# Three weight loads of the first dense layer asked for between the tiles of the attention's start

## The chip, the cores and the metric

The kernel runs on one core of one Trainium2 chip. The metric is the time of one execution on the device, in microseconds (us), the median of the runs shown. The core has a matrix engine (PE, with its weight loads as PEld), a vector engine (DVE), a scalar engine (ACT), a general engine (POOL) and a sync engine (SP), which here issues every transfer. Each engine takes its instructions from one queue, in order.

## The reference

An attention with 32 memory slots per head, then two dense layers, all in float32 (the weights of the dense layers come as float64):

```python
a = softmax(phi)                                  # (8, 8, 576, 32), over the 32 slots
k_m, v_m = a^T k, a^T v                           # (8, 8, 32, 64)
attn = softmax(q k_m^T / 8)                       # (8, 8, 576, 32)
x = (attn v_m) as (4608, 512)
h = max(x w1, x w2, x w3)                         # moe1: w1..w3 are 512 x 768
x = h w_out                                       # 768 x 512
x = (sigmoid(x w_gate) * (x w_val)) w_out         # moe2: 512 x 1536, 512 x 1536, 1536 x 512
```

## The kernel before

**The tiles.** The 8 x 8 heads are cut into 16 attention tiles, n = 2b + g: batch b, half g of the heads. Two batches make a pass p, so the first four tiles (n = 0 to 3) belong to pass 0. A tile goes through six stages, one generator each: `a0` (softmax of phi, begun), `a1` (it is transposed on PE), `a2` (k_m and v_m, PE matmuls at L209 from the tile's phi, k and v), `a3` (transposes at L228, then the splits into `vt` on ACT and DVE), `a4` (q k_m^T at L246, two halves of q; DVE transposes the scores at L256 and takes their maximum; POOL subtracts it, ACT takes the exponential) and `a5` (sum, division, transposed back into `stg`).

**The dense layer moe1.** Its weights w1, w2, w3 lie in `wx` as J = 6 column blocks of four row blocks (j, hp), 24 pieces of 128 x 384 float64, called w0 to w23 here in the order in which they are used (the fourth to sixth are w3, w4, w5). The values of v_m are multiplied into the weights first (`g_step`, PE at L343, results `g` split by ACT and DVE or POOL), and the attention is then multiplied with that (`h_step`, PE at L370).

**A weight's way.** `w_want` asks for a piece (tile `raw`, three buffers, 384 KB each). `w_have` turns it into float32 (`w_f32`, L123 to L129: two operations on ACT, three on DVE), splits it into a high and a low part (`w_split`: L134 on ACT, L73 on POOL) and stores both in `wxs` for the later passes (384 KB again). `w_step` asks for the next piece and then does `w_have` for the oldest one asked for; `wq` holds those asked for.

**What sets the order.** The first pass has a list `acts` of what is done ahead of step t of the first four tiles. Its transfers stay on SP in the order in which the program names them (`dma` with `queue["in order"]`); the other engines' instructions are put in order by a scheduler that works through a timeline of its own. All SP transfers share eight semaphores, so a transfer is issued when the one eight places ahead has landed. Tiles `early` (phi, q, k, v of the first tiles) have buffers of their own; from q of tile 1 on, `q` has three buffers.

After the list, the rest of the weights is stepped through at fixed places of the loop over pass 0 (`at(4 * (j - 2) + hp, w_step)`), beside `g_step` and `h_step`. After pass 0 there are three more passes, and then moe2.

Of the kernel before, what the change touches and what calls it, by code (L numbers as in the profile page):

```python
# [18 lines left out]
def attn_moe_kernel(  # L19
# [274 lines left out]
    def w_want(j, hp, p):  # L294
        if p == 0:
            wq.append((j, hp, p, w_fetch(mid, wx[j, hp] if j >= 0 else wo1[hp])))
        else:
            t = mid.tile([128, 2, PC], F32R, tag="wx", name="wx", bufs=6)
            dma(f32(t), wxs[j, hp])
            wq.append((j, hp, p, t))  # L300

    def w_have():
        j, hp, p, w = wq.pop(0)
        if j < 0:
            w = w_f32(mid, w)
            r = slice(hp * PC, hp * PC + PC)
            w_split(w, wo1_t[:, 0, r], wo1_t[:, 1, r])
            return
        if p == 0:
            w = w_f32(mid, w)  # L310
            t = mid.tile([128, 2, PC], F32R, tag="wx", name="wx", bufs=6)
            w_split(w, t[:, 0], t[:, 1])
            dma(wxs[j, hp], f32(t))
            w = t
        WX[j, hp] = w
# [213 lines left out]
    for pos, fn, *a in (  # L529
        (0, lambda: w_want(*w0[0])), (0, lambda: w_want(*w0[1])),  # L530
        (0, load_phi, 0), (0, load_kv, 0), (0, lambda: w_want(*w0[2])),
        (0, load_phi, 1), (0, load_kv, 1),
        (0, load_phi, 2), (0, load_phi, 3), (1, load_kv, 2), (2, load_kv, 3),
        *((n, load_q, n, e) for n in range(4) for e in range(2)),
        *((n + 1, lambda: w_step()) for n in range(4)),
    ):
        acts.setdefault(pos, []).append((fn, a))
    w0 = [(j, hp, 0) for j in range(J) for hp in range(4)]
# [2 lines left out]
    def w_step():  # L541
        if not wq:
            return
        if plan:
            w_want(*plan.pop(0))
        w_have()
# [337 lines left out]
```

## Time and profile before

| | |
|---|---|
| median of 3 runs | 1384.53 us (1384.27 to 1385.37) |
| the profiled execution's own time | 1385.23 us |
| its span | 1383.4 us |
| PE busy | 1336.3 us, 97% of the span |
| DVE busy | 862.3 us, 62% |
| mean granted clock of PE | 0.985 of full speed |

The times of rows are counted from the span's start. A row of the timeline gives start, duration, engine, line, operation, written tile, read tiles, shape and count, and in brackets the idle time of the engine just before it and what ended it. A row of a window gives, for each engine, its busy time there and in brackets how many instructions; PEclk is the granted clock of PE as a share of full speed, and the DMA share is the mean busy share of the 16 transfer engines. A row of several instructions covers the time from the first to the last of them.

### The profile page before, as it was taken

What the parts mean: (1) busy time and instruction counts of PE and PEld (TensorE: products, weight loads), DVE (VectorE), ACT (ScalarE), POOL (GpSimd) and SP (SyncE); (2) the same over time, 40 slices, a digit from 0 to 9 for tenths busy, and PEclk for the clock granted to TensorE, in tenths of its full rate; (3) what the DMA queues carried; (4) which work ended last, traced back from release to release, by engine and by line L of the source; (5) the groups of instructions that cost most, each with busy time, mean ns of one, the idle gap of its engine ahead of it and who ended that gap; (6) DMA issues with size and microseconds to landing.
All of it is one profiled execution on the core that took longest, in us unless ns stands there. A gap on an engine that the chain in (4) does not pass through costs nothing.

```text
span 1383.4 us, 22155 instructions
## 1 busy us (share of the span) xinstructions
PE 1336.3 (97%) x7864; PEld 1184.9 (86%) x7864; DVE 862.3 (62%) x1533; ACT 573.5 (41%) x1220; POOL 517.2 (37%) x454
## 2 busy tenths in 40 slices
PE   6689999998999999999999999999999999999998
PEld 3578899997999899888888888888888899999997
DVE  5999758877876885666665344553444544544454
ACT  5687546546654664453343311333222332233221
POOL 2775422421341228554586111461112711161111
PEclk9799999999999999999999999999999999999999
DMA  9588857579648935965556544565555676566661
GB/s 313 178 274 302 267 163 236 175 230 327 217 129 275 318 105 163 334 256 191 199 205 221 189 158 152 171 214 179 168 179 165 204 238 217 196 228 237 207 216 58
DMA packets 112270, 292.44 MB, mean 211 GB/s; under 512 B 12576, under 2 KB 28960, under 8 KB 112160
## 3 DMA queue, kind: packets, MB, share of 16 engines
q1 hardware_dynamic: 112160, 291.03, 62.5%
q8 instruction: 62, 1.02, 0.3%
q14 instruction: 48, 0.39, 0.1%
HBM read 224.92 MB, written 66.06 MB: 210 GB/s over the span
## 4 chain that ended last, share of the span: by engine, by line
PE 83%; DMA 7%; DVE 5%; ACT 2%; issue 2%; SPq 1%; POOL 0%; DVEq 0%; ACTq 0%
PE po L769 22%; PE px L702 16%; PE ps L370 13%; PE pv L702 10%; PE pz L702 10%; PE ps L393 7%; DMA raw<-wb_dram 3%; PE ps L343 2%; PE ps L246 1%; PE ps L209 1%; DMA raw<-wx_dram 1%; DMA early<-kvt_dram 1%; DVE ca L129 1%; DVE ca L128 1%; DVE g L73 1%
## 5 line engine op out<-in xcount | busy, mean ns | idle before, releaser
L769 PE MATMUL po<-wo,gg 128*128 128x512 f32 x1296 | 327.7, 392 | 1.0 <-POOL gg L73 1.0
L73 POOL TENSOR_TENSOR gg<-gf,gg 128x512 fp32r<-128x512 f32 (+1 forms) x120 | 143.4, 1195 | 468.9 <-ACT gg L735 426.0
L769 PEld LDWEIGHTS po<-wo,gg 128*128 128x128 f32 x1296 | 242.4, 188 | 49.5 <-POOL gg L73 1.3
L370 PE MATMUL ps<-attn,g 128*128 128x288 f32 x1728 | 258.9, 303 | 20.8 <-DVE g L73 9.4
L370 PEld LDWEIGHTS ps<-attn,g 128*128 128x128 f32 x1728 | 246.2, 194 | 30.0 <-POOL g L73 7.5
L702 PE MATMUL px<-xa,tb 128*128 128x512 f32 (+1 forms) x1080 | 243.7, 368 | 0.0
L781 DVE TENSOR_TENSOR acc<-po,acc 128x512 f32<-128x512 f32 x180 | 124.3, 691 | 175.0 <-PE po L769 174.9
L702 PEld LDWEIGHTS px<-xa,tb 128*128 128x128 f32 x1080 | 198.1, 188 | 28.0
L702 PE MATMUL pz<-xa,tb 128*128 128x512 f32 (+1 forms) x720 | 169.0, 367 | 1.1 <-DVE u L753 1.1
L702 PE MATMUL pv<-xa,tb 128*128 128x512 f32 (+1 forms) x720 | 169.2, 367 | 0.0
L393 PE MATMUL ps<-h,wo 128*128 128x288 f32 x1152 | 158.5, 296 | 0.0
L393 PEld LDWEIGHTS ps<-h,wo 128*128 128x128 f32 x1152 | 154.3, 188 | 2.8 <-issue 2.1
L73 POOL TENSOR_TENSOR h<-hm,h 128x288 fp32r<-128x288 f32 x96 | 84.1, 878 | 190.1 <-ACT h L68 98.3
L702 PEld LDWEIGHTS pz<-xa,tb 128*128 128x128 f32 x720 | 132.0, 188 | 20.0 <-issue 1.5
L702 PEld LDWEIGHTS pv<-xa,tb 128*128 128x128 f32 x720 | 131.8, 188 | 17.8
L735 ACT CAST gg<-gf 128x512 fp32r<-128x512 f32 (+1 forms) x120 | 69.4, 578 | 176.0 <-DVE gf L731 131.0
L753 DVE TENSOR_TENSOR u<-pz,p 128x512 f32<-128x512 f32 (+1 forms) x120 | 76.2, 635 | 100.8 <-PE pz L702 96.1
L725 ACT ACTIVATE sg<-sg 128x512 f32<-128x512 f32 (+1 forms) x90 | 53.1, 590 | 145.1 <-DVE sg L723 144.9
L73 DVE TENSOR_TENSOR g<-ps,g 64x384 fp32r<-64x384 f32 x180 | 99.3, 552 | 19.6 <-ACT g L357 16.4
L357 ACT CAST g<-ps 64x384 fp32r<-64x384 f32 x192 | 90.6, 473 | 45.6 <-DVE g L73 28.1
L73 POOL TENSOR_TENSOR xa<-xf,xa 128x512 fp32r<-128x512 f32 (+1 forms) x64 | 78.9, 1254 | 20.4 <-ACT xa L134 20.3
L731 DVE TENSOR_TENSOR gf<-gf,sg 128x512 f32<-128x512 f32 (+1 forms) x90 | 71.0, 789 | 9.9 <-ACT sg L725 1.3
(92 smaller groups left out, 1394.2 us busy)
## 6 DMA issues: line engine op xcount, KB each, us to landing
tb<-tbs SPq DMA_DIRECT2D x168, 512.0 KB, 3.8
wx<-wxs SPq DMA_DIRECT2D x72, 384.0 KB, 4.2
wo<-wos SPq DMA_DIRECT2D x48, 512.0 KB, 5.2
tbs<-tb SPq DMA_DIRECT2D x42, 512.0 KB, 2.9
raw<-wb_dram SPq DMA_DIRECT2D x48, 384.0 KB, 4.5
kv<-kvm_dram SPq DMA_DIRECT2D x48, 256.0 KB, 5.2
raw<-wx_dram SPq DMA_DIRECT2D x24, 384.0 KB, 3.7
wxs<-wx SPq DMA_DIRECT2D x24, 384.0 KB, 4.5
```

The source lines that it names most:

```text
L73: eng.tensor_tensor(out=o, in0=a, in1=b, op=ALU.subtract)
L343: pe.matmul(ps[:, :384], lhsT=vt[:, x, 2 * e:2 * e + 2].rearrange("p a m -> p (a m)"), rhs=w[:, y], start=(n == 0), stop=(n == 2),)
L357: act.copy(t[r, 0], ps[r, :384])
L370: pe.matmul(ps[w][:, :U], lhsT=G[b, j, g][:, x, 128 * w:128 * w + 128], rhs=at[:, y, hf * U:hf * U + U], start=(n == 0), stop=(n == 5),)
L393: pe.matmul(ps[:, :U], lhsT=wo1_t[:, x, (d * J + j) * 128:(d * J + j) * 128 + 128], rhs=H[u, j][:, y], start=(n == 0), stop=(n == 3 * J - 1),)
L702: pe.matmul(ps[:, :half], lhsT=w[:, a, o:o + 128], rhs=x[:, k, c, :half], start=(first and n == 0), stop=(n == 5), skip_group_check=not first,
L725: act.activation(out=sg, in_=src, func=AF.Sigmoid)
L731: vec.tensor_tensor(out=gf, in0=gf, in1=sg, op=ALU.mult)
L735: act.copy(t[:, 0, :half], gf)
L753: vec.tensor_tensor(out=u, in0=ps[:, :half], in1=E["p1", v], op=ALU.add)
L769: pe.matmul(ps, lhsT=GG[sc, j, c, h][:, x, 128 * m:128 * m + 128], rhs=WO[sc, j, h][:, y], start=(n == 0), stop=(n == 5),)
L781: vec.tensor_tensor(out=t, in0=ps, in1=t, op=ALU.add)
```

## The change

Three of the four calls of `w_step` in the list `acts` are moved ahead. The first now stands behind k and v of tile 1, ahead of phi of tiles 2 and 3; the second ahead of k and v of tile 2; the third ahead of k and v of tile 3. The fourth stays behind the loads of q. Each call asks for the next piece, converts the oldest one and stores it, so that loads, conversions and stores move together: w3 is asked for as w0 is converted and stored, w4 with w1, w5 with w2, w6 with w3.

```diff
         (0, load_phi, 0), (0, load_kv, 0), (0, lambda: w_want(*w0[2])),
-        (0, load_phi, 1), (0, load_kv, 1),
-        (0, load_phi, 2), (0, load_phi, 3), (1, load_kv, 2), (2, load_kv, 3),
+        (0, load_phi, 1), (0, load_kv, 1), (0, lambda: w_step()),
+        (0, load_phi, 2), (0, load_phi, 3), (1, lambda: w_step()), (1, load_kv, 2),
+        (2, lambda: w_step()), (2, load_kv, 3),
         *((n, load_q, n, e) for n in range(4) for e in range(2)),
-        *((n + 1, lambda: w_step()) for n in range(4)),
+        (3, lambda: w_step()),
     ):
```

SP's queue behind k and v of tile 1, before (`raw` is a weight's load, `wxs` a weight's store, `early` the first tiles' phi, q, k and v):

```order
L53 DMA early<-phiT_dram 128x576 x2
L53 DMA early<-qT_dram 128x576 x2
L53 DMA early<-kvm_dram 128x512 x4
L53 DMA early<-kvt_dram 64x512
L53 DMA q<-qT_dram 128x576 x2
L53 DMA raw<-wx_dram 128x384
L53 DMA wxs<-wx 128x768
L53 DMA early<-kvm_dram 128x512 x4
L53 DMA early<-kvt_dram 64x512
```

The same place now:

```order
L53 DMA raw<-wx_dram 128x384
L53 DMA wxs<-wx 128x768
L53 DMA early<-phiT_dram 128x576 x2
L53 DMA early<-qT_dram 128x576 x2
L53 DMA raw<-wx_dram 128x384
L53 DMA wxs<-wx 128x768
L53 DMA early<-kvm_dram 128x512 x4
L53 DMA early<-kvt_dram 64x512
L53 DMA q<-qT_dram 128x576 x2
L53 DMA raw<-wx_dram 128x384
L53 DMA wxs<-wx 128x768
L53 DMA early<-kvm_dram 128x512 x4
```

One weight's load and store stood ahead of k and v of tile 3; now there are three loads and three stores.

SP's queue at the last loads of q, now (q_216 and q_218 belong to tile 2, q_264 and q_266 to tile 3; wx_522 is w4 split, wx_547 is w5 split, wx_277 is w3 split; raw_268 is w6):

```order
L53 DMA q_216<-qT_dram 128x576
L53 DMA wxs_58<-wx_522 128x768
L53 DMA q_218<-qT_dram 128x576
L53 DMA q_264<-qT_dram 128x576
L53 DMA wxs_58<-wx_547 128x768
L53 DMA q_266<-qT_dram 128x576
L53 DMA raw_268<-wx_dram 128x384
L53 DMA wxs_58<-wx_277 128x768
L53 DMA raw_513<-wx_dram 128x384
```

The stores of w4 and w5 now stand between the loads of q, the one of w5 directly ahead of the second half of tile 3's q.

DVE's queue, before, from the conversion of w4 to the scores of tile 3 (ca_515 is w4, ca_540 is w5; s_464 are the scores of tile 2, s_493 those of tile 3):

```order
L127 TENSOR_SCALAR ca_515<-ca_515 128x384
L73 TENSOR_TENSOR vt_381<-ps_461,vt_381 128x64
L256 STREAM_TRANSPOSE s_464<-ps_455 128x288
L256 STREAM_TRANSPOSE s_464<-ps_456 128x288
L273 RECIPROCAL sm_448<-sm_448 128x18
L128 ISA ca_515<-ca_515,cr_516 128x768
L261 TENSOR_REDUCE mx_467<-s_464 128x18
L129 SCALAR_TENSOR_TENSOR ca_515<-raw_194,ca_515 128x384
L127 TENSOR_SCALAR ca_540<-ca_540 128x384
L276 STREAM_TRANSPOSE stg_453<-s_429 128x576
L128 ISA ca_540<-ca_540,cr_541 128x768
L129 SCALAR_TENSOR_TENSOR ca_540<-raw_255,ca_540 128x384
```

The rows that stand between w4's new place and w5's last operation, now, in two pieces; first w4 (s_372 are the scores of tile 0):

```order
L200 COPY es_332<-ps_306 64x128
L127 TENSOR_SCALAR ca_515<-ca_515 128x384
L128 ISA ca_515<-ca_515,cr_516 128x768
L129 SCALAR_TENSOR_TENSOR ca_515<-raw_146,ca_515 128x384
L256 STREAM_TRANSPOSE s_372<-ps_335 128x288
```

and then from w5 to the scores of tile 3 (s_429 are the scores of tile 1, g1_527 is a result of `g_step`):

```order
L129 SCALAR_TENSOR_TENSOR ca_540<-raw_193,ca_540 128x384
L271 TENSOR_REDUCE sm_448<-s_429 128x18
L276 STREAM_TRANSPOSE stg_397<-s_372 128x576
L272 TENSOR_SCALAR sm_448<-sm_448 128x18
L273 RECIPROCAL sm_448<-sm_448 128x18
L276 STREAM_TRANSPOSE stg_453<-s_429 128x576
L256 STREAM_TRANSPOSE s_464<-ps_455 128x288
L256 STREAM_TRANSPOSE s_464<-ps_456 128x288
L73 TENSOR_TENSOR vt_381<-ps_461,vt_381 128x64
L261 TENSOR_REDUCE mx_467<-s_464 128x18
L73 TENSOR_TENSOR vt_381<-ps_461,vt_381 128x64
L73 TENSOR_TENSOR g1_527<-ps_551,g1_527 64x384
```

The next row there is the first transpose of s_493. Both conversions that stood between the scores of tiles 2 and 3, or around them, now stand ahead of the scores of tile 2, and one split of `g` has come ahead of the scores of tile 3. On PE, five `g_step` (15 matmuls at L343) now stand between the two halves of tile 3's q product (L246), where there were four (12). The order of the engines differs only in pass 0: PE's queue is word for word the same from about its 322nd row of 2270 to the end (that row lies in the `x2_step` part of pass 0, L393).

## Rows read from the trace of the kernel before

**Rows 1.** The page: busy time of PE and of DVE, and the granted clock of PE, in 40 slices of the span.

```profile
PE   6689999998999999999999999999999999999998
DVE  5999758877876885666665344553444544544454
PEclk9799999999999999999999999999999999999999
```

**Rows 2.** Windows of the whole span.

```profile
0.00:35.00 35.00, 21.85 (x215) 11.74 (x216) 18.55 (x51) 18.86 (x48) 8.07 (x13) 0.90 0.93 311
35.00:137.00 102.00, 82.35 (x550) 74.41 (x547) 100.28 (x185) 77.53 (x183) 70.37 (x63) 0.87 0.75 250
137.00:200.00 63.00, 63.00 (x505) 56.97 (x506) 41.69 (x94) 28.99 (x70) 24.73 (x22) 1.00 0.67 218
600.00:1383.40 783.40, 778.40 (x3653) 671.52 (x3651) 399.63 (x604) 224.45 (x406) 268.58 (x225) 1.00 0.56 192
```

**Rows 3.** Windows of the first 50 us.

```profile
10.00:20.00 10.00, 8.47 (x101) 5.47 (x101) 5.84 (x19) 6.60 (x18) 1.34 (x2) 1.00 1.05 365
20.00:30.00 10.00, 7.13 (x91) 3.37 (x89) 6.07 (x17) 4.24 (x13) 1.78 (x2) 0.89 1.05 348
30.00:35.00 5.00, 4.90 (x29) 1.99 (x22) 1.57 (x4) 2.31 (x7) 2.60 (x3) 0.53 0.65 228
35.00:40.00 5.00, 4.16 (x22) 2.75 (x18) 5.00 (x11) 2.50 (x7) 4.00 (x3) 1.00 0.97 323
45.00:50.00 5.00, 0.61 (x2) 0.64 (x3) 4.94 (x10) 4.83 (x12) 4.42 (x5) 0.50 0.55 215
```

**Rows 4.** The chain that ended last, in order of time, the transfers of the first tiles in it (start, duration, what).

```profile
4.01 6.43 DMA early<-kvt_dram
10.46 5.89 DMA early<-phiT_dram
16.37 6.11 DMA early<-kvt_dram
22.50 7.13 DMA early<-kvm_dram
```

**Rows 5.** Groups of DVE instructions by line from 0 to 34 us, the three of the conversion (busy time, mean ns of one; idle before them and its releaser).

```profile
L128 DVE CUSTOM_DVE_ANT_0 ca<-ca,cr 128x768 uint16<-128x768 uint16 x4 | 2.7, 674 | 0.1
L129 DVE SCALAR_TENSOR_TENSOR ca<-raw,ca 128x384 uint32<-128x384 uint32 x4 | 2.2, 555 | 0.1
L127 DVE TENSOR_SCALAR ca<-ca 128x384 uint32<-128x384 uint32 x4 | 1.4, 358 | 7.1 <-ACT ca L123 7.1
```

**Rows 6.** The same three groups from 34 to 145 us.

```profile
L129 DVE SCALAR_TENSOR_TENSOR ca<-raw,ca 128x384 uint32<-128x384 uint32 x25 | 21.9, 878 | 0.3
L128 DVE CUSTOM_DVE_ANT_0 ca<-ca,cr 128x768 uint16<-128x768 uint16 x25 | 19.4, 779 | 0.2
L127 DVE TENSOR_SCALAR ca<-ca 128x384 uint32<-128x384 uint32 x25 | 17.2, 692 | 0.1
```

**Rows 7.** Timeline of DVE from w4's conversion to the transposes of tile 3's scores and the split after them.

```profile
35.19 0.35 DVE L127 TENSOR_SCALAR ca<-ca 128x384 uint32<-128x384 uint32 x1
35.45 0.22 DVE L73 TENSOR_TENSOR vt<-ps,vt 128x64 fp32r<-128x64 f32 x1
...
36.49 1.35 DVE L128 CUSTOM_DVE_ANT_0 ca<-ca,cr 128x768 uint16<-128x768 uint16 x1
37.77 0.74 DVE L261 TENSOR_REDUCE mx<-s 128x18 f32<-128x576 f32 x1
38.43 0.85 DVE L129 SCALAR_TENSOR_TENSOR ca<-raw,ca 128x384 uint32<-128x384 uint32 x1
39.20 1.31 DVE L127 TENSOR_SCALAR ca<-ca 128x384 uint32<-128x384 uint32 x1
40.43 0.77 DVE L276 STREAM_TRANSPOSE stg<-s 128x576 f32<-128x576 f32 x1
41.13 0.66 DVE L128 CUSTOM_DVE_ANT_0 ca<-ca,cr 128x768 uint16<-128x768 uint16 x1
41.82 1.24 DVE L129 SCALAR_TENSOR_TENSOR ca<-raw,ca 128x384 uint32<-128x384 uint32 x1
42.98 0.83 DVE L256 STREAM_TRANSPOSE s<-ps 128x288 f32<-128x288 f32 x2
43.75 0.51 DVE L73 TENSOR_TENSOR g<-ps,g 64x384 fp32r<-64x384 f32 x1
```

**Rows 8.** Timeline of PE and, at its end, of ACT: tile 3's k and v (L209), its transposes (L228), the q products of tiles 2 and 3 (L246; eight records are a tile's product), the first `g_step` (L343), the first `h_step` (L370), and ACT's copy between L209 and L228; and, at the top, a q product earlier on.

```profile
18.83 1.20 PE L246 MATMUL ps<-early,kt 128*64 128x288 f32 x8
...
29.67 1.40 PE L209 MATMUL ps<-early,es 128*32 128x128 f32 x16
33.11 0.69 PE L228 MATMUL ps<-ident,kvb 128*128 128x128 f32 x2
33.73 1.91 PE L246 MATMUL ps<-q,kt 128*64 128x288 f32 x8
35.57 2.36 PE L343 MATMUL ps<-wx,vt 128*128 128x384 f32 x12
37.86 1.18 PE L246 MATMUL ps<-q,kt 128*64 128x288 f32 x4
...
49.39 2.50 PE L370 MATMUL ps<-attn,g 128*128 128x288 f32 x9 [7.05 <-DVE g L73]
...
31.19 0.63 ACT L218 ACTIVATE kvb<-ps,rm 128x128 f32<-128x128 f32 x2 [1.32 <-PE ps L209]
```

**Rows 9.** SP's queue in the first 62 us: whom its transfers waited for (us in total, times, the longest).

```profile
SPq L53 <- POOL wx L73: 6.4, 3, 3.7
```

## The prediction

> **What bounds the kernel now.** I read the page's slices first. PE is full nearly everywhere; it is not in the first slices, and there DVE stands at 9 [rows 1]. The windows say where the bound changes. From 35 to 137 us DVE is busy for 100.28 of 102 us, and PE for only 82.35; from 137 to 200 us PE is busy for 63.00 of 63, and from 600 us to the end for 778.40 of 783.40 [rows 2]. So there are three stretches: a start of 35 us in which neither is full (DVE 18.55 us of 35, that is 16.45 us idle), a stretch of 102 us that DVE sets, and the rest, which PE sets. What DVE reaches earlier in the second stretch, PE gets earlier, and with the same order of instructions behind it the end comes earlier by as much.
>
> What bounds the start is the third thing to read. The transfer engines show a share of 1.05 from 10 to 30 us, at 365 and 348 GB/s [rows 3], and the chain that ended last is four transfers of the first tiles in a row from 4 to 29.6 us [rows 4]. So the start is set by bytes, and DVE waits for them. The change gives DVE work for this idle time, and puts bytes in front of the tiles to do so. The question is which is larger.
>
> **What is removed.** In the changed order the conversions of w4 and w5 stand ahead of the scores of tile 2; before, they lay on both sides of them. I count what they hold of DVE up to the transposes of tile 3's scores at 42.98, each from its start to the start of the next row [rows 7]. w4: 35.45 - 35.19 = 0.26, 37.77 - 36.49 = 1.28, 39.20 - 38.43 = 0.77, together 2.31. w5: 40.43 - 39.20 = 1.23, 41.82 - 41.13 = 0.69, 42.98 - 41.82 = 1.16, together 3.08. Sum 5.39 us of the 7.79 between 35.19 and 42.98. If DVE alone set that point, it would come at 42.98 - 5.39 = 37.6.
>
> **What this adds in the start.** There a conversion takes DVE (1.4 + 2.7 + 2.2) / 4 = 1.58 us [rows 5], so the two take 3.2 us of the 16.45 that are idle. The work of ACT (two operations and a cast) and POOL (a split) goes with them; ACT is busy for 18.86 of these 35 us and POOL for 8.07 [rows 2], and I cost both at nothing. If that cover fails, it is one conversion's 1.58 us. w3 also moves, but it was converted before 35 us in either order, and the wait of DVE for it lay in a time that the tiles' transfers set: nothing.
>
> **What the bytes cost.** Ahead of k and v of tile 3 stand the loads of w4 and w5 and the stores of w1 and w2 in addition (w3 and the store of w0 stood there before). That is four transfers of 384 KB, 0.393 MB each. At the mean of 365 and 348 GB/s [rows 3] one is 1.10 us and the four are 4.4 us. Nothing hides that, since the transfer engines are full there: tile 3's value matmuls, which ended at 29.67 + 1.40 = 31.07 [rows 8], end at 35.5.
>
> The Trainium skill's page "DMA: Bandwidth & Descriptors", section "Bandwidth", has 425 GB/s for one large transfer by a single core. No row of the first 30 us reaches that; by it the four would cost 3.7 us, and the point below would come 0.7 us earlier.
>
> **The chain behind them.** From 35.5 on, ACT's copy takes 0.63 and the transposes 0.69 [rows 8]: 36.8. Then PE has the second half of tile 2's q product and the first of tile 3's, fifteen matmuls of `g_step`, and the second half of tile 3's product. The fifteen cost 15 x 2.36 / 12 = 2.95. The halves cost 1.91 for two and 1.18 for the last as they stand here, or 0.60 each as an earlier product (1.20 for eight records) did [rows 8]; the granted clock was 0.53 from 30 to 35 us, behind a stretch with idle gaps, and 1.00 from 35 to 40 [rows 3]. So the product of tile 3 ends between 36.8 + 1.2 + 2.95 + 0.6 = 41.5 and 36.8 + 1.91 + 2.95 + 1.18 = 42.8. I take the middle, 42.2, since there will be idle gaps here too. It is later than the 37.6 of DVE alone, so now DVE waits for PE at the transposes, and the point moves from 42.98 to 42.2, by 0.8 us. One split of `g`, which followed at 43.75 and took 0.51 [rows 7], is done by then in the changed order: it fills part of that wait.
>
> **The sum.** 0.8 + 0.5 = 1.3 us gained when DVE's full stretch goes on, and carried to the end. The profiled execution took 1385.23, 1.83 more than its span of 1383.4, and becomes 1383.9. The median shown is 0.70 below it, so I predict 1384.53 - 1.3 = 1383.2.
>
> The bounds of the chain: at best nothing of it is later than DVE, and the gain is 5.4. At worst all of the 39.04 - 31.07 = 7.97 us that lay between the end of the value matmuls and that of the product stays (37.86 + 1.18 = 39.04) [rows 8], its waits included: 35.5 + 8.0 = 43.4, which with the split ahead is no gain and no loss.
>
> **The rivals.** What this measurement can tell from no change is about 0.2%, 2.8 us.
>
> *The tiles' lag is covered.* Before, tile 3's product ended at 39.04 [rows 8] and DVE read it at 42.98 [rows 7], 3.9 us later. So most of a lag of 4.4 us falls into a time in which the product lay waiting. If PE's part shrinks with the full clock and the transfers run a little faster, DVE alone decides, and 3 to 5.4 us are gained: 1379.1 to 1381.5, say 1380.5. Against it: the transfers are full, and PE's queue now has three more `g_step` matmuls ahead of the second half. Rows speak for a high price of a conversion in the crowded stretch: its three operations take 878 + 779 + 692 = 2349 ns from 34 us on [rows 6] against 1.58 us before that, with POOL busy for 70.37 of 102 us [rows 2]. The Trainium skill's page "SBUF — State Buffer", section "SBUF: two separate sides", says that POOL and some DVE operations exclude each other for a whole instruction; by that rule the excess is POOL's holding time, which stays and falls on other DVE instructions, and only 2 x 1.58 = 3.2 us would be gained at best. The difference between the two rows agrees with it, but cannot show where the excess goes.
>
> *The two cancel.* The lag takes all that the conversions give: 1384.5. For it: in the start DVE idled for 7.1 us ahead of three conversions [rows 5], waits that lay beside the tiles' own; moving them changes nothing as long as the tiles' bytes set the pace, and there are more of these. Against it: DVE's queue had a backlog at 35 us, and it has less to do now.
>
> *SP stands at a store.* The store of w5 now stands directly ahead of the second half of tile 3's q, and of the load of w6. It waits for POOL's split, which comes behind DVE's third operation. SP's longest wait for such a split was 3.7 us [rows 9]. Ahead of that q half there is also one transfer more than I counted for the values, the store of w5 itself, 1.1 us. If both come on top, the product ends at 42.2 + 3.7 + 1.1 = 47.0, that is 4.0 later than DVE read it, less the 0.5 of the split: 3.5 slower, 1388.0. It decides as soon as that q half lands later than about 45.7 (42.98 + 2.8 + 0.5 - 0.6 for the half product). For it: w5's conversion stands in DVE's queue among the scores of tile 1, whose own waits hold it. Against it: w5's load is asked for some 4 us ahead of the q loads, and POOL is idle for most of the start.
>
> **Chances.** My forecast (0.3 to 2.7 us faster) 0.36, the lag covered 0.30, the two cancel 0.16, SP at the store 0.18. The second is faster by over 0.2%, the last slower; the first and the third lie within: 0.30, 0.52, 0.18. For the range I leave out the best end of the second and the worst of the last: 1379.9 to 1387.2. The forecast's own is 1381.8 to 1384.2.
>
> **What would show it.** In the changed profile: conversions of w4 and w5 before 35 us, at about 1.6 us each; DVE busy for some 3 us more in the first 35 us than 18.55; the last value matmuls of the first four tiles at about 35.5 in place of 31.07; DVE idle, released by PE, ahead of the transposes of tile 3's scores at about 42; the first `h_step` on PE one to two us ahead of 49.39 [rows 8]; and from 200 us on PE's rows with the same gaps, shifted. I am wrong if the value matmuls come much later or earlier than 35.5, if SP waits for POOL ahead of the last q, or if DVE is idle between 50 and 137 us for more than the 1.7 us of before.

## The result and the profile after

| | before | changed |
|---|---|---|
| median of six runs each | 1384.40 us (1383.26 to 1385.61) | 1393.33 us (1389.43 to 1393.75) |
| span of the profiled execution | 1383.4 us | 1391.4 us |
| end of the first four tiles' value matmuls | 31.07 us | 35.30 us |
| DVE begins the transposes of tile 3's scores | 42.98 us | 47.20 us |
| first `h_step` on PE | 49.39 us | 53.31 us |
| first matmul of `x2_step` (L393) | 149.10 us | 157.14 us |

The ratio is 1.0056, with a 95% interval from 1.0045 to 1.0067. The forecast was 1383.2 us, with a range of 1379.9 to 1387.2: the change is slower, and the time lies outside the range. Here and below, medians and ratios leave out four lone slow executions (1476 to 3377 us), which moves a median by about 0.5 us at most, so that 1385.86 in an expectation is 1385.46 here.

The last two rows of the table show when the time is lost: 3.9 us by the first `h_step`, 8.0 us by the first `x2_step`, and 8.0 us at the end of the span. Taken together, nothing more is lost or won after 157 us.

Windows of the changed kernel, in the columns of [rows 2] and [rows 3]: the window and its length, the busy time of PE, PEld, DVE, ACT and POOL, the granted clock, the DMA share and GB/s.

```profile
0.00:35.00 35.00, 19.17 (x199) 10.66 (x202) 19.39 (x53) 18.93 (x47) 8.21 (x14) 0.85 0.98 328
35.00:137.00 102.00, 78.33 (x484) 68.45 (x483) 90.68 (x170) 72.32 (x168) 65.39 (x60) 0.87 0.67 230
...
30.00:35.00 5.00, 3.74 (x46) 1.45 (x46) 3.80 (x10) 2.28 (x8) 1.82 (x3) 1.00 1.05 341
35.00:40.00 5.00, 2.14 (x16) 0.91 (x12) 3.66 (x7) 2.26 (x5) 3.55 (x4) 1.00 0.42 154
40.00:45.00 5.00, 4.85 (x16) 2.42 (x15) 2.44 (x6) 1.68 (x6) 3.79 (x3) 0.66 0.97 304
```

The second row is the finding. DVE was full from 35 to 137 us, idle for 102 - 100.28 = 1.72 us [rows 2]; now it is idle for 102 - 90.68 = 11.3 us. The hole begins at once: from 35 to 40 us PE is busy for 2.14 of 5 us, DVE for 3.66, ACT for 2.26, and the transfers stand at 0.42. From 40 to 45 PE is nearly full at a granted clock of 0.66, and DVE falls to 2.44. Engines wait for one another there, and the next views say in which order.

PE's timeline from the end of the value matmuls to the first `h_step`, to be read beside [rows 8]:

```profile
34.88 0.42 PE L209 MATMUL ps<-early,es 64*32 64x128 f32 x8 [0.22 <-DMA early<-kvt_dram]
35.42 1.16 PE L246 MATMUL ps<-q,kt 128*64 128x288 f32 x4
39.31 0.44 PE L228 MATMUL ps<-ident,kvb 128*128 128x128 f32 x2 [2.73 <-ACT kvb L218]
39.68 1.77 PE L246 MATMUL ps<-q,kt 128*64 128x288 f32 x4
41.60 2.13 PE L246 MATMUL ps<-q,kt 128*64 128x288 f32 x4 [0.15 <-ACT kt L231]
43.66 2.87 PE L343 MATMUL ps<-wx,vt 128*128 128x384 f32 x15
46.46 1.19 PE L246 MATMUL ps<-q,kt 128*64 128x288 f32 x4
53.31 2.50 PE L370 MATMUL ps<-attn,g 128*128 128x288 f32 x9 [5.66 <-DVE g L73]
```

The values end at 34.88 + 0.42 = 35.30, close to the 35.5 of the forecast. PE then does the first half of tile 2's q product, to 36.58, and the transposes behind it (L228) wait 2.73 us for ACT's copy, where the forecast had 0.63 for the copy in all. ACT's timeline says what it did in that time:

```profile
36.71 0.51 ACT L134 CAST wx<-ca 128x384 fp32r<-128x384 f32 x1 [1.16 <-DVE ca L129]
38.06 0.67 ACT L284 CAST attn<-stg 128x576 fp32r<-128x576 f32 x1 [0.83 <-DVE stg L276]
38.64 0.62 ACT L218 ACTIVATE kvb<-ps,rm 128x128 f32<-128x128 f32 x2
40.71 0.67 ACT L284 CAST attn<-stg 128x576 fp32r<-128x576 f32 x1 [1.46 <-DVE stg L276]
41.29 0.26 ACT L231 COPY kt<-ps 128x128 f32<-128x128 f32 x1
```

ACT did little in that time; it waited. Its queue holds the cast of w5 (L134), which waits 1.16 us for DVE's last operation on w5, then the cast of tile 0's attention (L284), which waits 0.83 us for DVE's transpose, and only then the copy of tile 3 (L218). The copy's data had been there since 35.30; it starts at 38.64, without any wait of its own. That is why it doesn't show as a waiting row on ACT: one sees it only as PE's wait. A second cast (L284, 1.46 us of waiting) stands ahead of tile 3's `kt`.

DVE's timeline of the same time, the conversion of w5 first:

```profile
33.47 0.35 DVE L127 TENSOR_SCALAR ca<-ca 128x384 uint32<-128x384 uint32 x1
...
33.99 1.26 DVE L128 CUSTOM_DVE_ANT_0 ca<-ca,cr 128x768 uint16<-128x768 uint16 x1
35.28 1.40 DVE L129 SCALAR_TENSOR_TENSOR ca<-raw,ca 128x384 uint32<-128x384 uint32 x1
36.60 0.74 DVE L271 TENSOR_REDUCE sm<-s 128x18 f32<-128x576 f32 x1
37.26 0.76 DVE L276 STREAM_TRANSPOSE stg<-s 128x576 f32<-128x576 f32 x1
...
39.90 0.78 DVE L276 STREAM_TRANSPOSE stg<-s 128x576 f32<-128x576 f32 x1 [1.27 <-POOL s L274]
...
46.37 0.55 DVE L73 TENSOR_TENSOR g<-ps,g 64x384 fp32r<-64x384 f32 x1 [3.48 <-ACT g L357]
47.20 0.97 DVE L256 STREAM_TRANSPOSE s<-ps 128x288 f32<-128x288 f32 x2 [0.28 <-PE ps L246]
```

w5's conversion, asked for ahead of tile 3, is what holds ACT first: it costs 0.35 + 1.26 + 1.40 = 3.0 us here, and ACT's cast can only follow its last operation, at 36.68. The cast of tile 0 then waits for the transpose of 37.26 to 38.02 (L276), which stands behind that conversion in DVE's queue. And DVE then stands 3.48 us ahead of the first split of `g`, because that split needs the `g_step` that PE reaches late.

DVE's longest waits from 35 to 150 us (in total, times, the longest):

```profile
DVE g L73 <- ACT g L357: 4.6, 3, 3.5
DVE ca L127 <- ACT ca L123: 2.4, 3, 0.9
DVE hm L381 <- PE ps L370: 1.3, 1, 1.3
DVE stg L276 <- POOL s L274: 1.3, 1, 1.3
```

In the kernel before, the longest of this view is 1.2 us. Last, SP's queue (start, duration, what) and its wait, to be read beside [rows 9]:

```profile
30.88 1.46 SPq L53 DMA_DIRECT2D q<-qT_dram  x2
38.32 0.33 SPq L53 DMA_DIRECT2D wxs<-wx  x1
38.75 0.37 SPq L53 DMA_DIRECT2D q<-qT_dram  x1
39.22 0.87 SPq L53 DMA_DIRECT2D raw<-wx_dram  x1
...
SPq L53 <- POOL wx L73: 8.1, 3, 5.8
```

SP stands at the store of w5 from 32.3 to 38.32 and cannot issue the last half of tile 3's q before 38.75, nor the load of w6 before 39.22 (34.58 before). This is the third rival, as it was described. PE uses that half of q only at 46.46, so SP's wait lies beside the one that begins on ACT, and only runs can tell which of them decides.

### The profile page after: what moved, and what is told of

Its sections match the earlier page's. It is cut to its first block, busy times and chain, and to the rows that moved or that the text cites. A ratio compares the mean times of both kernels' runs of the same rounds, so it can differ in the third digit from the quotient of the medians.

```text
span 1391.4 us, 22156 instructions
## 1 busy us (share of the span) xinstructions
PE 1336.7 (96%) x7864; PEld 1185.7 (85%) x7864; DVE 859.3 (62%) x1533; ACT 573.2 (41%) x1220; POOL 515.2 (37%) x454
## 4 chain that ended last, share of the span: by engine, by line
PE 82%; DVE 7%; DMA 6%; issue 2%; ACT 2%; POOL 0%; SPq 0%; DVEq 0%; ACTq 0%
PE po L770 21%; PE px L703 16%; PE ps L370 12%; PE pz L703 11%; PE pv L703 10%; PE ps L393 6%; PE ps L343 2%; DMA raw<-wb_dram 2%; DVE ca L129 1%; PE ps L246 1%; PE ps L209 1%; DVE g L73 1%; DVE ca L128 1%; DVE ca L127 1%; DMA raw<-wx_dram 1%
## 5 line engine op out<-in xcount | busy, mean ns | idle before, releaser
L370 PE MATMUL ps<-attn,g 128*128 128x288 f32 x1728 | 257.8, 303 | 18.6 <-DVE g L73 8.0
L370 PEld LDWEIGHTS ps<-attn,g 128*128 128x128 f32 x1728 | 246.3, 194 | 27.0 <-POOL g L73 6.1
L393 PE MATMUL ps<-h,wo 128*128 128x288 f32 x1152 | 158.1, 296 | 0.0
L393 PEld LDWEIGHTS ps<-h,wo 128*128 128x128 f32 x1152 | 154.2, 188 | 2.3 <-issue 1.3
```

The costliest lines, as they stand in the source:

```text
L370: pe.matmul(ps[w][:, :U], lhsT=G[b, j, g][:, x, 128 * w:128 * w + 128], rhs=at[:, y, hf * U:hf * U + U], start=(n == 0), stop=(n == 5),)
L393: pe.matmul(ps[:, :U], lhsT=wo1_t[:, x, (d * J + j) * 128:(d * J + j) * 128 + 128], rhs=H[u, j][:, y], start=(n == 0), stop=(n == 3 * J - 1),)
```

## The experiments

Three groups of runs, each beside its own runs of the kernel before. "Values", "scores", `h` and `x2` are the four points of the table above, in the profiled execution. Two profiled executions of the changed kernel, that of the table above and that of "the change again", differ by 0.4 to 1.1 us at these points, so smaller differences between rows say nothing.

| run | median, us | ratio to before, 95% interval | values | scores | h | x2 |
|---|---|---|---|---|---|---|
| first call moved alone | 1390.83 | 1.0037 [1.0022, 1.0051] | 32.03 | 43.94 | 54.58 | 155.36 |
| first two moved | 1385.22 | 1.0004 [0.9989, 1.0019] | 32.82 | 40.43 | 47.69 | 147.60 |
| all moved, three stores later | 1380.10 | 0.9965 [0.9952, 0.9979] | 32.89 | 39.88 | 44.42 | 144.62 |
| change, ACT's copy first | 1385.46 | 0.9994 [0.9981, 1.0007] | 34.76 | 43.06 | 49.99 | 149.42 |
| the change again | 1391.27 | 1.0050 [1.0034, 1.0067] | 35.65 | 46.61 | 52.71 | 156.01 |
| change, two stores behind a load | 1389.49 | 1.0029 [1.0016, 1.0042] | 35.34 | 44.73 | 51.65 | 151.30 |
| stores later, bytes put back | 1385.27 | 1.0008 [0.9993, 1.0022] | 36.02 | 45.48 | 49.41 | 147.28 |
| stores later and copy first | 1381.10 | 0.9970 [0.9960, 0.9980] | 31.64 | 39.44 | 43.85 | 147.78 |
| first alone, w6 and w7 pinned | 1383.22 | 0.9982 [0.9969, 0.9995] | 30.45 | 42.40 | 47.74 | 144.98 |
| before, w6 and w7 pinned | 1383.60 | 0.9988 [0.9974, 1.0001] | 31.61 | 43.52 | 48.45 | 149.01 |
| change, w6 and w7 pinned | 1388.41 | 1.0017 [1.0007, 1.0027] | 35.07 | 47.54 | 51.54 | 153.30 |
| copy first, w6 and w7 pinned | 1385.99 | 1.0005 [0.9995, 1.0016] | 34.54 | 42.36 | 47.78 | 152.41 |

The medians of before beside the first four, the next four and the last four are 1385.72, 1384.79 and 1385.39 us.

### The calls one by one

Only the first call moved, the other two back behind the loads of q:

```diff
-        (0, load_phi, 2), (0, load_phi, 3), (1, lambda: w_step()), (1, load_kv, 2),
-        (2, lambda: w_step()), (2, load_kv, 3),
+        (0, load_phi, 2), (0, load_phi, 3), (1, load_kv, 2), (2, load_kv, 3),
...
-        (3, lambda: w_step()),
+        *((n + 1, lambda: w_step()) for n in range(1, 4)),
```

> Only the first of the three calls is moved (w3's load and w0's store ahead of phi of tiles 2 and 3); the others stand where they stood. k and v of tile 3 then have as many transfers ahead of them as in the kernel before, those of tile 2 two more. Bytes theory (the loss is the lag of the last tile's k and v): last value matmuls near 31, time within 1 us of before, 1383.5 to 1385.5. Queue theory (the loss comes from w5's conversion and the casts that stand ahead of tile 3's copy in ACT's queue): w5 is converted where it was, so also no loss. If this one is 3 us or more slower, both are wrong.

And the first two:

```diff
-        (2, lambda: w_step()), (2, load_kv, 3),
+        (2, load_kv, 3),
...
-        (3, lambda: w_step()),
+        *((n + 1, lambda: w_step()) for n in range(2, 4)),
```

> The first two calls are moved, the third not. Ahead of k and v of tile 3 stand two transfers more than in the kernel before, not four, and w5 is converted at its old place, behind tile 3's copy. Bytes theory: half of the loss, 1388 to 1390, last value matmuls near 33.3. Queue theory: the copy follows the value matmuls at once, loss at most the part of 2.2 us that the backlog does not take, 1384 to 1386.

The steps don't add up, and neither theory had the first. The first alone costs 5.1 us (1390.83 beside 1385.72), though its values are only 1 us late and PE's L228 waits for nobody. The first two together cost nothing that can be measured, with the second's two transfers more; that is the time of the queue theory. So there is a cost that has to do neither with bytes nor with the wait of ACT's copy. It shows on DVE, which is full in this run from 35 us to the first `h_step`. DVE's timeline of the first call alone:

```profile
49.59 0.48 DVE L73 TENSOR_TENSOR g<-ps,g 64x384 fp32r<-64x384 f32 x1
50.00 1.30 DVE L127 TENSOR_SCALAR ca<-ca 128x384 uint32<-128x384 uint32 x1
51.23 1.34 DVE L129 SCALAR_TENSOR_TENSOR ca<-raw,ca 128x384 uint32<-128x384 uint32 x1
52.50 1.34 DVE L128 CUSTOM_DVE_ANT_0 ca<-ca,cr 128x768 uint16<-128x768 uint16 x1
53.87 1.04 DVE L73 TENSOR_TENSOR g<-ps,g 64x384 fp32r<-64x384 f32 x2
```

and of the kernel before:

```profile
47.65 0.54 DVE L128 CUSTOM_DVE_ANT_0 ca<-ca,cr 128x768 uint16<-128x768 uint16 x1
48.11 1.13 DVE L73 TENSOR_TENSOR g<-ps,g 64x384 fp32r<-64x384 f32 x2
```

Three operations of w6 and w7 have come ahead of the pair of splits that the first `h_step` waits for. They hold that pair for 53.87 - 50.00 = 3.9 us, and PE waits 10.96 us ahead of that `h_step`, 7.05 before [rows 8]. w6 and w7 aren't needed there; this order is the scheduler's. The last group of runs tests this.

### The bytes, ACT's queue, SP's queue

The three calls stay moved, but the stores of w0, w1 and w2 are held back until the last q is asked for; loads and conversions stand as in the change (the third call and the end of the list are shown; the first two calls are edited alike):

```diff
-        (2, lambda: w_step()), (2, load_kv, 3),
+        (2, lambda: w_step(held)), (2, load_kv, 3),
...
+        (3, lambda: w_store()), (3, lambda: w_store()), (3, lambda: w_store()),
         (3, lambda: w_step()),
```

> The change with the stores of w0, w1 and w2 put behind the last loads of q. Ahead of k and v of tile 3 stand w3, w4 and w5 and no store, one transfer more than before the change. Bytes theory: last value matmuls near 32.2, most of the loss gone, 1384 to 1387. Queue theory: w5's cast still stands ahead of tile 3's copy in ACT's queue, so the copy waits as in the changed kernel (it began at 38.64), and the time stays at 1390 to 1393.

This is faster than both kernels, 1380.10 us, 0.35% below before, and faster than either theory had it. Its first stretch and three rows of DVE:

```profile
0.00:35.00 35.00, 20.39 (x210) 11.31 (x211) 22.41 (x58) 21.28 (x52) 10.70 (x16) 0.95 0.94 307
...
41.55 1.47 DVE L73 TENSOR_TENSOR g<-ps,g 64x384 fp32r<-64x384 f32 x3
...
43.71 1.51 DVE L73 TENSOR_TENSOR g<-ps,g 64x384 fp32r<-64x384 f32 x3
...
45.93 0.36 DVE L127 TENSOR_SCALAR ca<-ca 128x384 uint32<-128x384 uint32 x1
```

DVE is busy for 22.41 us of the first 35 there (18.55 before [rows 2]): the conversions did go into the idle start, and all six splits of `g` stand ahead of w6's conversion. So the idea behind the prediction pays once the stores don't stand ahead of tile 3.

Next, the change with ACT's order mended: w5's conversion and the cast of tile 0 are queued behind tile 3's copy.

```diff
+            queue["kvb", n] = act.activation(
+                out=kvb[:, :, e], in_=p[:, :128].rearrange("p (x d) -> p x d", x=2),
+                func=AF.Copy, scale=st["rm"][:, e:e + 1])
...
+            if (j, hp) == (1, 1):
+                with tc.issue_after(queue["kvb", 3].ins):
+                    w = w_f32(mid, w)
...
-            a_split(t - len(stages) + 1)
+            with tc.issue_after(queue["kvb", 3].ins):
+                a_split(t - len(stages) + 1)
```

> The change with the same transfers ahead of the tiles, but w5's conversion and the cast of tile 0's result kept behind tile 3's copy in ACT's queue. Bytes theory: last value matmuls still near 35.3, so the loss stays, 1390 to 1393. Queue theory: the copy begins within 0.5 us of the value matmuls' end, near 35.8 in place of 38.64, the first h_step some 2 to 3 us ahead of 53.3, and the time is 1387 to 1390.

The transfers ahead of tile 3 are those of the change, the values end at 34.76, and the time is back at that of before, below what either theory had. ACT's timeline of this run:

```profile
34.88 0.63 ACT L218 ACTIVATE kvb<-ps,rm 128x128 f32<-128x128 f32 x2 [0.41 <-PE ps L209]
```

The copy starts as soon as PE is done, 3.8 us earlier than in the change, and the scores of tile 3 are read 4.1 us earlier. By the ratios, each to its own runs of before, the edit is worth (1.0050 - 0.9994) x 1385 = 7.8 us. It doesn't change ACT's order alone. w5's conversion moves on DVE, and with it w5's store on SP: it goes out at 43.87, behind the last half of tile 3's q (37.15) and the load of w6 (37.57), where the change had it ahead of both.

The change was then run again, beside three more:

> The changed kernel once more, beside the other runs of this call on the same chip, since executions of one kernel were seen to spread by some us from chip to chip. Every theory: 0.4 to 0.7% slower than the kernel before, value matmuls' end near 35.3, first h_step near 53.

It repeats, at 1.0050. SP's wait at the stores was tried by queuing the stores of w4 and w5 behind the next load of a weight, with the loads of q ahead of them:

```diff
-            dma(wxs[j, hp], f32(t))
+            if (j, hp) in ((1, 0), (1, 1)):
+                later(dma, wxs[j, hp], f32(t))
+            else:
+                dma(wxs[j, hp], f32(t))
```

> The change with the stores of w4 and w5 queued behind the next load of a weight on SP, so that the second half of tile 3's q and the load of w6 no longer stand behind w5's store (SP waited up to 5.8 us for POOL there). Store theory (my rival: SP stands at w5's store and what is behind it comes late): the last q half and w6's load are issued some 5 us earlier, the time falls by 2 to 4 us, to 1388 to 1391. Queue theory: tile 3's copy still waits behind the casts in ACT's queue and the first h_step stays within 1 us of 53.3; the time stays within 2 us of the changed kernel.

SP's longest wait for POOL's split falls from 5.8 to 0.7 us, and the time by 1.8 us in the medians (1389.49 beside 1391.27), or (1.0050 - 1.0029) x 1385 = 2.9 us by the ratios. The intervals of the two overlap, and both theories allowed such a time. The last half of q and the load of w6 go out only 1.3 us earlier (37.48 and 37.91), not 5, since SP now waits up to 4.0 us for an earlier transfer of q and 2.4 us for PE's q product. So the store's wait lay beside others of the same queue. ACT's copy still starts 1.8 us behind the values (37.17 against 35.34), behind the same two casts, and PE waits 1.80 us for ACT's `kt` ahead of tile 3's product. The store on SP was a real wait, and not the one that decided. It bounds what its move can have given in the run with ACT's copy first: up to 2.9 of the 7.8 us, which leaves some 5 for ACT's order and w5's later conversion, an estimate, since the parts need not add up. (The profiled execution of this run, at 1385.22 us, was its fastest, so the positions in its row may be early ones.)

To part the bytes from the rest, the faster version got three copies of 384 KB within DRAM where the stores had stood (the output is the full one, the copies are extra; the first of the three is shown):

```diff
-        (0, load_phi, 1), (0, load_kv, 1), (0, lambda: w_step(held)),
+        (0, load_phi, 1), (0, load_kv, 1), (0, lambda: w_step(held)), (0, extra, 0),
```

> The kernel with the three stores put later (1380.1, 0.35% faster than before), and in place of each store a copy of the same 384 KB from one place of the chip's memory to another, which nothing waits for. Its output is complete; the copies are extra work. Bytes theory (the three transfers ahead of the last tiles are what turns the gain into a loss, through the lag and the order that the scheduler makes of it): value matmuls' end goes from 32.9 back to 35 to 36, and the time to 1388 to 1394, like the change. If it is the stores themselves (their wait for POOL's split, the buffers they hold), the time stays at 1380 to 1384.

The values are late again (36.02). By the ratios (1.0008 - 0.9965) x 1385 = 6.0 us come back, of (1.0050 - 0.9965) x 1385 = 11.8 between that version and the change. In this run ACT's two casts stand ahead of the copy again, which starts 1.4 us behind the values (37.42). So these 6 us are the bytes together with what a late tile 3 meets in ACT's queue. The time lies between the ranges of the two theories. The other half isn't the lateness of the values, which end no earlier here than in the change. Here w6's conversion begins at 50.16, behind all the splits that the first `h_step` (49.41) needs; in the change it begins at 49.19, ahead of two of them. The last group of runs shows what that order can be worth.

> The three stores put later, and tile 3's copy kept ahead of w5's conversion and of the cast of tile 0's result in ACT's queue. If lag and queue each cost something of their own, this is the fastest, 1376 to 1380. If the queue costs only where the lag has already moved tile 3's copy behind the casts, it is within 2 us of the kernel with the stores put later, 1378 to 1382, or slower, since w5 is converted later.

With the stores later, ACT's order is worth nothing that can be measured: 1381.10 beside 1380.10, with ratios of 0.9970 and 0.9965. There the values end early, and the copy starts 0.1 us behind them even without this edit (33.00 against 32.89). ACT's queue costs time only when tile 3 is late, so the prices of the two can't be added.

### The place of w6 and w7

Four kernels with one edit: the conversions of w6 and w7 are pinned on DVE behind the last split of the first four `g_step`. The loads and stores that these two calls ask for move behind it with them (`queue["g"]` is the latest split of `g` on DVE; the line that notes it is not shown).

```diff
     for hp in range(4):
-        w_step()
+        if hp < 2:
+            w_step()
         run(g_step(0, 0, hp))
-    for hp in range(4):
-        w_step()
+    for hp in range(6):
+        if hp < 2:
+            with tc.issue_after(queue["g"].ins):
+                w_step()
+        else:
+            w_step()
```

> Edit: only the first call moved, as in the run with the first alone (1390.83 beside 1385.72 us), and the conversions of w6 and w7 pinned on DVE behind the last split of the first four g_step. Theory (the place of these two conversions among the first splits is what cost 5 us there): the split that the first h_step needs comes at about 49 in place of 53.87 us, the first h_step at 48 to 50 in place of 54.58, and the kernel is within 2 us of the one before. Rival (the place only moves the wait; the same DVE work stands ahead of the first x2_step, L393): the first h_step comes earlier, but the first x2_step stays at about 155 us and the kernel at 1389 to 1391.

> Edit: the kernel before, with the conversions of w6 and w7 pinned on DVE behind the last split of the first four g_step. Theory (such a place is worth time where DVE is the bound): in the kernel before, w6's L127, L128 and w7's L127 stand among these splits already, 1.3 + 0.5 + 0.3 us by the trace, so the first h_step comes 0.5 to 2 us ahead of 49.40; the kernel is 0 to 2 us faster than before. Rival (any new order here costs as the first alone did): slower by 3 us or more.

> Edit: the change, with the conversions of w6 and w7 pinned on DVE behind the last split of the first four g_step. Theory (the change's 8 us are about 5 of bytes and ACT's queue and a part for this place): first h_step at 50 to 52 in place of 52.7 to 53.3, the kernel at 1386 to 1390, that is 1 to 5 us better than the change. Rival (the place is of no account here, since DVE waits for tile 3 anyway): 1390 to 1393.5.

> Edit: the change with ACT's copy of tile 3 ahead of w5's conversion and the cast of tile 0 (1385.86 us alone), and the conversions of w6 and w7 pinned on DVE behind the last split of the first four g_step. Theory (the two are separate): first h_step 0.5 to 2 us ahead of the 49.99 of that run and the kernel at 1383 to 1385.5. Rival (the pin only moves a wait): 1385.5 to 1387.

The first kernel settles the surprise of the run with the first call alone: 1383.22 us, (1.0037 - 0.9982) x 1385 = 7.6 us less than without the pin, and 2.2 below the kernel before. DVE's timeline of it:

```profile
46.52 2.03 DVE L73 TENSOR_TENSOR g<-ps,g 64x384 fp32r<-64x384 f32 x4
48.58 0.61 DVE L127 TENSOR_SCALAR ca<-ca 128x384 uint32<-128x384 uint32 x1
```

The splits run in one piece and the first `h_step` starts at 47.74 in place of 54.58, a little earlier than the theory's 48 to 50. The kernel before gains 1.8 us in the medians by the same edit, as expected, though its interval just reaches 1. (Its profiled execution was the fastest of its runs, so its positions are early ones.) The change gains (1.0050 - 1.0017) x 1385 = 4.6 us by the ratios; its `h` (51.54) and its time are where the theory put them. But at its first `h_step` it isn't w6's one operation ahead of the splits that costs: that one (L127 at 49.19) holds DVE for 0.3 us. One row of DVE in the change stands out:

```profile
50.11 2.00 DVE L272 TENSOR_SCALAR sm<-sm 128x18 f32<-128x18 f32 x1
```

and the same operation in the pinned change:

```profile
50.19 0.16 DVE L272 TENSOR_SCALAR sm<-sm 128x18 f32<-128x18 f32 x1
```

In the change it runs while POOL has two operations back to back, from 49.97 to 52.08, and ends with them; in the pinned kernel POOL's next operation starts only at 50.41. The 1.84 us between the two rows are about what the first `h_step` gains (1.77); no run takes this wait away by itself. So it isn't only the count of operations ahead of a split that sets its time, but also what POOL does beside them.

With ACT's copy first and the pin, the rival held: the first `h_step` comes 2.2 us earlier, but the first `x2_step` 3 us later, and the time is 1385.99, the same as without the pin within the intervals (1.0005 beside 0.9994). There the pin only moved a wait.

## Why the prediction was wrong

**The bound of the start, and the price of the bytes: right.** Four transfers of 384 KB were to delay the values from 31.07 to 35.5; they ended at 35.30. The transfers stood at a share of 1.05 from 10 to 35 us, at 341 GB/s in the last five of them and 383 in the best five. The Trainium skill's page "DMA: Bandwidth & Descriptors", section "Bandwidth", states 425 GB/s for one large transfer. No window there came near it, and the trace's own rate gave the better sum.

**The conversions in the idle start: half right.** w3 and w4 were converted at 18.3 and 23.8 us for 0.36 + 0.56 + 0.56 = 1.5 us each. w5 came only at 33.47 and cost 3.0, the crowded price of [rows 6], not 1.58. DVE's busy time in the first 35 us rose by 19.39 - 18.55 = 0.8 us, not by 3, since the tiles' own work left that stretch as they were delayed.

**The chain behind the values: the step that failed.** "ACT's copy takes 0.63 and the transposes 0.69" counted the copy's duration and not its place in the queue, and the work of ACT for the conversions was costed "at nothing" because ACT is busy for only 18.86 of 35 us. The place was what counted. For a cover by ACT that fails the prediction had 1.58 us; the wait for the copy alone was 2.73. From the values to the end of L228 the forecast had 1.3 us, and it took 39.75 - 35.30 = 4.45. It also left out the first half of tile 2's q product, which PE does in between (35.42 to 36.58); by itself that would have put the end of the transposes at about 37.0, so it is not what failed. The two q halves were given 1.55 in the middle of the bounds and took (41.60 + 2.13) - 39.75 = 4.0 us, with a granted clock of 0.66 from 40 to 45 us (a mean of stretches at 1.2 and at 2.4 GHz, behind five us in which PE was busy for only 2.14) and a gap of 0.15 for `kt`. The fifteen `g_step` took 2.9 as forecast, the last half 1.1 against 0.9. Less the 0.2 us by which the values came early, that is 5.4 us: the product of tile 3 ended at 47.65, not 42.2. The run with the copy first confirms the first of these, and takes back all of the loss, with w5's store and conversion later as well. The worst bound given, 43.4, was too low for the same reason. It let old waits stay, but left no room for new ones on ACT.

**DVE's full stretch from 35 us on: failed.** It was the premise by which a gain at 42 us was carried to the end. DVE has 9.6 us more idle time from 35 to 137 us, and 5.8 us in place of 1.6 from 50 to 137, which the prediction had named as a sign of being wrong, like SP's wait for POOL ahead of the last q. 5.5 us of the idle time lie ahead of the first `h_step` (1.27 + 3.48 + 0.28 in the rows shown, and 0.44 ahead of tile 2's transposes), by the chain above. The rest comes behind it, up to 157 us. From the first `h_step` to the first `x2_step` it is 99.7 us in the kernel before, 103.8 in the change and 101.8 in the change pinned. The pinned kernel thus gets back half of that second part, so a part of it is the place of w6 and w7 in DVE's queue. The load of w6, asked for 4.6 us later (39.22), does not explain the remainder: in the run with the bytes put back it goes out at 42.98, and that stretch takes 97.9 us. What the remainder is stays open.

**The rivals.** The third, SP at w5's store, described the right direction and a true wait (5.8 us, longer than the 3.7 it was priced at), and its 1388.0 was the nearest of the four times. But moving that store behind the loads returned 1.8 us in the medians and 2.9 by the ratios, and ACT's copy was still 1.8 us late without it. "The lag is covered" assumed that the product would lie waiting for DVE, and it was DVE that waited. "The two cancel" is near what the change gives once ACT's copy goes first (a ratio of 0.9994). The forecast had no rival for the order itself: it took DVE's order behind tile 3 as given, although the place of w6's and w7's operations among the splits was worth 7.6 us in one of the runs.

**What stays open.** Three causes are shown by runs that take each away: the stores' bytes ahead of tile 3, ACT's casts ahead of its copy (together with w5's later conversion and store), and w6 and w7 among the first splits. Each of these runs also alters the order elsewhere, and they overlap: taking away the second and the third together gave no more than the second alone. A split of the 8 us into three sums isn't supported.

## What to carry to other kernels

When work is moved into another engine's idle time, follow every engine that the work passes through, and look in each queue at what stands behind it. An instruction that waits for its data holds what is queued behind it: ACT's casts held tile 3's copy for 3.3 us here, with ACT busy for 1.35 of these 3.3. Move the loads and conversions that are needed early, and leave stores that nobody waits for behind the loads that are waited for: that turned 0.5% slower into 0.35% faster here. And where a scheduler sets the order, read the new order at the points that the next stage waits for, also where the edit did not touch it.

## What the runs showed of the hardware

The same three operations of a conversion took 1.5 us on DVE at 18 and 24 us, and 3.0 us at 33 us, with DVE waiting for nothing between them. A DVE operation of 128x18 took 2.00 us beside two operations of POOL, and 0.16 us in another run where POOL started behind it. The copy that ACT's queue held from 35.30 to 38.64 has a row without any idle time of its own; it shows only as PE's wait of 2.73 us. The kernel with the first call alone changed by 7.6 us with the place of two conversions in DVE's queue, at the same work, and with DVE idle for less than 0.1 us from 35 us to the first `h_step` in both.
